# Attention followed by two dense layers: splits and value products put behind given instructions of their own engine

## The chip, the cores and the metric

One core of a Trainium2 chip. The kernel is one program; the metric is device time in microseconds, the median of several executions. The profile is one execution of its own, taken by the hardware profiler. Engines are named as in the profile: PE is TensorE (PEld its weight loads), DVE is VectorE, ACT is ScalarE, POOL is GpSimd, SP is SyncE, which here only issues transfers.

## The reference

Attention with a mask by hash bucket, and two dense blocks behind it:

```
q_bits = (q @ proj > 0); k_bits = (k @ proj > 0)          # 6 bits a row
mask   = bucket(q_bits) == bucket(k_bits)
scores = where(mask, q @ k.T / sqrt(64), -1e9)
attn   = softmax(scores); x = attn @ v                    # 2 batches, 8 heads, 768 rows, 64 wide
h  = x @ w_in;  g  = where(h > 0, h, exp(min(h, 0)) - 1);  x2 = g @ w_out     # 1536 x 512, inner 2048
h2 = x2 @ w_in2; g2 = s * relu(h2)**2 + b;                 out = g2 @ w_out2
```

## The kernel before

All large products keep the precision of 32 bits by splitting an operand into a high and a low 16-bit part and adding three products. The weights arrive as 64-bit numbers and are joined to 32-bit words on DVE (lines 213, 214, 216, one chunk is these three), then split (lines 205, 206, 221, 223).

The attention works in units. A unit is one head and 128 query rows: `u_s` makes its 128 x 768 scores on PE (line 384), `u_soft` takes their maximum on DVE (395, 396) and the exponential on ACT (397), `u_split` and `u_av` multiply by the values. There are 96 units; 16 of them are the first two chunks of rows, which `unit` orders so that units 0 to 3 are chunk 0 of heads 0 to 3, units 4 to 7 chunk 1 of the same heads, and units 8 to 15 the same for heads 4 to 7. For these 16, `u_split` transposes the exponentials on PE (line 406, six matmuls of 32-bit data), copies them out (line 409 on ACT), and `u_av` multiplies them with the raw 32-bit values (line 434). From unit 16 on the exponentials are split into two halves on ACT (416) and POOL (419), transposed by a DMA from SP (421), and multiplied with split values (440).

Heads come in four pairs. Before a pair's first unit its keys and queries are split by `p_split` (lines 280 or 282 the high part, 297 a copy, 285 the remainders), transposed by DMAs (303, 304, 312), hashed by `p_bits` (matmuls of line 340, comparison on DVE in line 343) and turned into buckets by `p_buck` (353, 357). `p_v` splits a pair's values for the units from 16 on (323 on ACT, 324 on DVE). Score tiles have one PSUM buffer in this stage, so a unit's scores wait for the maximum of the unit before.

What runs when is set in two steps. The tables at the head of the file (`SPLIT0`, `BITS0`, `PV0`, `LOADV`) say behind which unit a step is written by `attention`, and the order in which the program is written gives every instruction a priority. A scheduler then builds each engine's queue from the priorities and its own estimate of times. Each engine works its queue in order, so an instruction that waits holds up all behind it. `tc.issue_after(x)` adds one constraint: what is written inside it stands behind `x` in the queue of `x`'s engine.

Alongside, `w_stream` brings the first layer's weights; `moe1` (574, 582 to 597) starts on the first two chunks when both are normalised by `u_norm` and transposed (479). From then on matmuls of the first layer alternate with attention units, and after the attention only dense layers are left.

Of the kernel before, what the change touches and what calls it, by code (L numbers as in the profile page):

```python
# [19 lines left out]
EX = dict(p=1, ph=1, pt=1, raw=2)  # L20
NP = 3
LOAD = [(-1, -1), (0, 0)]
SPLIT0 = [(-4, -4), (-3, -3), (1, 1), (2, 3)]
ENG0 = ['dve', 'act', 'act', 'act']
MXP = 44
BITS0 = [-2, -1, 4, 6]
BUCK0 = [1, 0, 1, 1]
LOADV = [1, 2, 5, 6]
WN = 1
# [34 lines left out]
W_FROM = 3  # L64
HOLD = {(0, 2, "v"): 3, (0, 3, "v"): 4, (1, 0, "k"): 8, (1, 0, "q"): 9}
HOLD_E = []
LN2 = 0.6931471805599453


def model_kernel(tc, q, k, v, proj, w_in, w_out, w_in2, w_out2, s2, b2, sel, pop, eye, out):  # L70
    nc = tc.nc
# [23 lines left out]
    with ExitStack() as base:  # L95
# [194 lines left out]
        def p_split(b, hp, nm, eng):  # L290
            t = raws.pop((b, hp, nm)).rearrange("p h (c d) -> p h c d", d=D)
            s_ = ring.take("ph", [128, 2, C, 2, D], F16, "src")
            full = lambda z: z.rearrange("p h c t -> p (h c) t")
            if nm == "k":
                hi = s_[:, :, :, 0, :]
                scaled(eng, hi, t, SQ)
                side(b, hp).tensor_copy(out=s_[:, :, :, 1, :], in_=hi)
                l_ = ring.take("ph", [128, C, 2, D], F16, "srcl")
                for j in range(2):
                    rest(l_[:, :, j, :], t[:, j], SQ, hi[:, j])  # L300
                o1 = per.tile([128, 2, C, 128], F16, tag=f"k1{hp}", name=f"k1{hp}")
                o2 = per.tile([128, 2, C, 128], F16, tag=f"k2{hp}", name=f"k2{hp}")
                nc.sync.dma_start_transpose(out=full(o1), in_=s_.rearrange("p h c x d -> p (h c x d)"))
                nc.sync.dma_start_transpose(out=o2[:, 0], in_=l_.rearrange("p c x d -> p (c x d)"))
                k1[b, hp], k2[b, hp] = o1, o2
                return
            for j in range(2):
                hi, lo = s_[:, j, :, j, :], s_[:, j, :, 1 - j, :]
                scaled(eng, hi, t[:, j], -SQ)
                rest(lo, t[:, j], -SQ, hi)  # L310
            o1 = per.tile([128, 2, C, 128], F16, tag=f"q1{hp}", name=f"q1{hp}")
            nc.sync.dma_start_transpose(out=full(o1), in_=s_.rearrange("p h c x d -> p (h c x d)"))
            o2 = per.tile([128, 2, C, 128], F16, tag=f"q2{hp}", name=f"q2{hp}")
            for j in range(2):
                side(b, hp).tensor_copy(out=o2[D * j:D * j + D, j], in_=o1[D * j:D * j + D, j])
            q1[b, hp], q2[b, hp] = o1, o2

        def p_v(b, hp):
            t = raws[b, hp, "v"]
            vv = per.tile([128, 2, C, 2, D], F16, tag=f"vv{hp}", name=f"vv{hp}")  # L320
            hi, lo = vv[:, :, :, 0, :], vv[:, :, :, 1, :]
            t = t.rearrange("p h (c d) -> p h c d", d=D)
            nc.scalar.activation(out=hi, in_=t, func=ACTF.Copy, scale=SV)
            nc.vector.scalar_tensor_tensor(out=lo, in0=t, scalar=SV, in1=hi, op0=ALU.mult, op1=ALU.subtract)
            vHL[b, hp] = vv

# [51 lines left out]
        def u_s(u):  # L378
            b, c, h, hp, j = unit(u)
            p = ps_s[0].tile([128, S], F32, tag="s", name="s")  # L380
            for x, (w, m) in enumerate(((q1, k1), (q2, k2))):
                kf = m[b, hp][:, j].rearrange("p c t -> p (c t)")
                for a0, a1 in halves:
                    nc.tensor.matmul(p[:, a0:a1], w[b, hp][:, j, c, :], kf[:, a0:a1],  # L384
                                     start=(x == 0), stop=(x == 1))
            sps[u] = p

        def u_soft(u):
            b, c, h, hp, j = unit(u)
            gr, sl = group(u)  # L390
            if sl == 0:
                sums[gr] = sml.tile([128, H], F32, tag="sum", name="sum")
            f = ring.take("p", [128, S], F32, "p")
            mx = sml.tile([128, 1], F32, tag="mx", name="mx")
            nc.vector.tensor_scalar(f, sps.pop(u), CLAMP, None, op0=ALU.min, op1=ALU.min, accum_out=mx)  # L395
            (nc.gpsimd if U0 <= u < MXP else nc.vector).tensor_scalar(mx, mx, sm / (SQ * SQ), 10.0 * LN2, op0=ALU.mult, op1=ALU.add)  # L396
            nc.scalar.activation(out=f, in_=f, func=ACTF.Exp, scale=-sm / (SQ * SQ), bias=mx,  # L397
                                 accum_out=sums[gr][:, sl:sl + 1])
            pf[u] = f

        def u_split(u, eng):
            f = pf.pop(u)
            if u < FC * H:
                p = ps_p[0].tile([128, S], F32, tag="s", name="pT")
                for cc in range(C):
                    nc.tensor.transpose(p[:, 128 * cc:128 * cc + 128], f[:, 128 * cc:128 * cc + 128], ident)  # L406
                o = ring.take("pt", [128, S], F32, "pt")
                if eng == "act":
                    nc.scalar.activation(out=o, in_=p, func=ACTF.Copy)
# [14 lines left out]
        def u_av(u):  # L424
# [6 lines left out]
            if u < FC * H:  # L431
                vv = raws[b, hp, "v"].rearrange("p h (c d) -> p h c d", d=D)
                for cc in range(C):
                    nc.tensor.matmul(acc, o[:, 128 * cc:128 * cc + 128], vv[:, j, cc, :],  # L434
                                     start=(cc == 0), stop=(cc == C - 1))
                return
            vv = vHL[b, hp]
            for z, (x, y) in enumerate(((0, 0), (0, 1), (1, 0))):
# [587 lines left out]
```

## Time and profile before

| | |
|---|---|
| median of 3 runs | 711.56 us (709.78 to 711.82) |
| profiled execution, its own time | 714.04 us |
| its span in the trace | 711.8 us |
| PE busy | 659.6 us, 93% of the span |
| DVE busy | 520.5 us, 73% |
| ACT busy | 416.3 us, 58% |
| POOL busy | 266.1 us, 37% |

The shares are means over stages with different limits; the span is read stage by stage, in forty slices of 17.8 us and in windows. The granted clock is a share of TensorE's full 2.4 GHz, so 0.50 is its lower level of 1.2 GHz. "Idle before" in brackets names what ended an engine's wait.

### The profile page before, as it was taken

The numbers are of one execution on the slowest core, as the hardware profiler recorded it, in microseconds if no ns is written. First come the engines' busy times: TensorE is split into PE (matmuls) and PEld (weight loads), VectorE is DVE, ScalarE is ACT, GpSimd is POOL, SyncE is SP. The second block draws the span as 40 slices with busy tenths as digits, with TensorE's granted clock in tenths as the row PEclk, the third lists the DMA queues.
The fourth block names the chain that finished last, engine by engine and source line by source line (L and its number), as shares of the span: only waits on it lengthen the run. The fifth ranks groups of instructions, "written<-read, shape, count | busy, mean of one in ns | idle before, by whom it ended". The sixth has DMA issues, their size and how long they took to land.

```text
span 711.8 us, 15212 instructions
## 1 busy us (share of the span) xinstructions
PE 659.6 (93%) x6192; PEld 506.6 (71%) x6192; DVE 520.5 (73%) x893; ACT 416.3 (58%) x687; POOL 266.1 (37%) x211
## 2 busy tenths in 40 slices
PE   2598978879989999999999999999999999999998
PEld 0286857668767777888888988874444446888887
DVE  5779989998878568645644699339999626999730
ACT  2849768966778788656755333234545525555520
POOL 0136767776345469945855421311211200000000
PEclk9769999999999999999999999999999999999999
DMA  9965699999999669977668555014443000000100
GB/s 211 299 162 170 160 203 203 223 228 225 196 211 216 116 116 171 150 125 122 119 115 117 135 162 165 1 31 119 135 138 112 0 1 1 16 31 31 45 30 30
DMA packets 206805, 89.72 MB, mean 126 GB/s; under 512 B 171920, under 2 KB 203408, under 8 KB 206736
## 3 DMA queue, kind: packets, MB, share of 16 engines
q1 hardware_dynamic: 206144, 88.63, 57.4%
q8 instruction: 48, 0.79, 0.5%
q14 instruction: 21, 0.17, 0.1%
q10 hardware_dynamic: 592, 0.14, 0.1%
HBM read 43.13 MB, written 3.15 MB: 65 GB/s over the span
## 4 chain that ended last, share of the span: by engine, by line
PE 66%; DMA 10%; DVE 10%; ACT 7%; issue 5%; SPq 1%; POOL 1%; DVEq 0%; ACTq 0%; POOLq 0%
PE h L574 27%; PE y L818 15%; PE x2p L574 12%; DMA pt<-ph 6%; PE s L384 4%; PE xacc L440 3%; PE xacc L434 2%; DVE p L395 2%; ACT p L397 1%; PE pT L406 1%; ACT ph L416 1%; DMA q<-src 1%; DVE g L591 1%; DMA raw<-in_k 1%; ACT q L357 1%
## 5 line engine op out<-in xcount | busy, mean ns | idle before, releaser
L419 POOL TENSOR_TENSOR ph<-p,ph 128x768 f16<-128x768 f32 x80 | 134.6, 1686 | 79.2 <-ACT ph L416 44.3
L574 PE MATMUL h<-x,wih 128*128 128x256 f16 x768 | 131.3, 275 | 3.0 <-DVE g L591 1.5
L574 PE MATMUL h<-x,wi 128*128 128x512 f16 x576 | 124.5, 379 | 0.0
L395 DVE TENSOR_SCALAR_CACHE_REDUCE p<-s 128x768 f32<-128x768 f32 x96 | 91.0, 951 | 42.2 <-PE s L384 41.3
L397 ACT ACTIVATE p<-p,mx 128x768 f32<-128x768 f32 x96 | 89.2, 929 | 50.6 <-DVE mx L396 38.8
L818 PE MATMUL y<-wqh,a 128*128 128x256 f16 x672 | 110.3, 273 | 0.0
L818 PEld LDWEIGHTS <-a 128*128 128x128 f16 x1008 | 98.6, 98 | 11.7
L574 PE MATMUL h<-x,wil 128*128 128x256 f16 x384 | 105.4, 275 | 0.0
L574 PE MATMUL x2p<-gh,woh 128*128 128x256 f16 x384 | 104.1, 273 | 0.8 <-ACT gh L594 0.8
L574 PE MATMUL x2p<-gl,woh 128*128 128x256 f16 x384 | 104.5, 273 | 0.1
L574 PEld LDWEIGHTS <-wi 128*128 128x128 f16 x576 | 56.4, 98 | 67.7
L574 PE MATMUL x2p<-gh,wol 128*128 128x256 f16 x384 | 104.5, 273 | 0.0
L818 PE MATMUL y<-wql,a 128*128 128x256 f16 x336 | 91.1, 273 | 0.0
L384 PE MATMUL s<-k,q 128*128 128x512 f16 (+1 forms) x384 | 80.7, 335 | 8.0 <-DVE p L395 7.9
L574 PEld LDWEIGHTS <-wih 128*128 128x128 f16 x768 | 74.9, 99 | 15.2 <-issue 2.0
L574 PEld LDWEIGHTS <-woh 128*128 128x128 f16 x768 | 74.9, 98 | 11.6
L597 POOL TENSOR_TENSOR gl<-g,gh 128x512 f16<-128x512 f32 x48 | 59.0, 1229 | 61.0 <-ACT gh L594 60.7
L440 PE MATMUL xacc<-vv,pt 128*128 128x64 f16 x1440 | 57.6, 194 | 16.1 <-DMA pt<-ph 16.1
L416 ACT ACTIVATE ph<-p 128x768 f16<-128x768 f32 x80 | 66.7, 836 | 7.7 <-DMA pt<-ph 5.2
L440 PEld LDWEIGHTS <-pt 128*128 128x128 f16 x1440 | 53.5, 99 | 24.3 <-DMA pt<-ph 20.3
L610 DVE SCALAR_TENSOR_TENSOR g<-h,sbs,r 128x512 f32<-128x512 f32 x48 | 35.7, 745 | 23.6 <-ACT r L607 23.6
L384 PEld LDWEIGHTS <-q 128*128 128x128 f16 x384 | 34.5, 100 | 25.6 <-issue 10.8
(118 smaller groups left out, 1040.8 us busy)
## 6 DMA issues: line engine op xcount, KB each, us to landing
wraw<-in_moe_w_in SPq DMA_DIRECT2D x32, 512.0 KB, 3.9
wraw<-in_moe_w_out SPq DMA_DIRECT2D x32, 512.0 KB, 3.9
out<-y SPq DMA_DIRECT2D x10, 256.0 KB, 2.0
raw<-in_k SPq DMA_DIRECT2D x6, 384.0 KB, 4.8
raw<-in_q SPq DMA_DIRECT2D x6, 384.0 KB, 5.7
v<-in_v SPq DMA_DIRECT2D x4, 384.0 KB, 7.8
pt<-ph SPq DMA_TRANSPOSE x80, 4.1
x<-in_k SPq DMA_DIRECT2D x2, 384.0 KB, 5.0
```

What stands on the lines that cost most here:

```text
L357: nc.scalar.activation(out=o[r, j].rearrange("p c t -> p (c t)"), in_=p[r], func=ACTF.Relu, scale=sc, bias=pop_sb[r, x:x + 1])
L384: nc.tensor.matmul(p[:, a0:a1], w[b, hp][:, j, c, :], kf[:, a0:a1], start=(x == 0), stop=(x == 1))
L395: nc.vector.tensor_scalar(f, sps.pop(u), CLAMP, None, op0=ALU.min, op1=ALU.min, accum_out=mx)
L397: nc.scalar.activation(out=f, in_=f, func=ACTF.Exp, scale=-sm / (SQ * SQ), bias=mx, accum_out=sums[gr][:, sl:sl + 1])
L416: nc.scalar.activation(out=t[:, 0, :], in_=f, func=ACTF.Copy)
L419: nc.gpsimd.tensor_tensor(out=t[:, 1, :], in0=f, in1=t[:, 0, :], op=ALU.subtract)
L434: nc.tensor.matmul(acc, o[:, 128 * cc:128 * cc + 128], vv[:, j, cc, :], start=(cc == 0), stop=(cc == C - 1))
L440: nc.tensor.matmul(acc, o[:, C * x + cc, :], vv[:, j, cc, y, :], start=(z == 0 and cc == 0), stop=(z == 2 and cc == C - 1))
L574: nc.tensor.matmul(p, ws[a](kk), xs[b](kk), start=(kk == 0 and z == 0), stop=(kk == n_kk - 1 and z == 2))
L597: nc.gpsimd.tensor_tensor(out=gl, in0=t["g"], in1=gh, op=ALU.subtract)
L610: nc.vector.scalar_tensor_tensor(out=g, in0=p, scalar=sb["s"], in1=t["r"], op0=ALU.mult, op1=ALU.mult)
L818: nc.tensor.matmul(p, a[:, xa, kk, :], wq[y][:, WQ[n], kk, :], start=first and k == 0, stop=k == 3 * K2 - 1, skip_group_check=True)
```

## The change

The fourth pair's splits are written behind units 4 and 5 instead of 2 and 3, and its bits one unit later. Five constraints are added: its key split stands behind the exponential of unit 1, the first half of its query split behind that of unit 2; the value splits of the first two pairs behind the exponentials of units 4 and 5; the value product of unit 0 behind the transposes of unit 2, and that of unit 1 behind the scores of unit 4. To be named in a constraint, exponentials, scores and transposes are kept in `pins`.

```diff
-SPLIT0 = [(-4, -4), (-3, -3), (1, 1), (2, 3)]
+SPLIT0 = [(-4, -4), (-3, -3), (1, 1), (4, 5)]
...
-BITS0 = [-2, -1, 4, 6]
+BITS0 = [-2, -1, 4, 7]
...
+HOLD_V = {0: 4, 1: 5}
+HOLD_A = {0: ("pT", 2), 1: ("s", 4)}
+HOLD_S = {(0, 3, "k"): 1, (0, 3, "q"): 2}
...
+            u_ = HOLD_S.get((b, hp, nm))
+            held = tc.issue_after(pins["exp", u_]) if u_ is not None else nullcontext()
             if nm == "k":
                 hi = s_[:, :, :, 0, :]
-                scaled(eng, hi, t, SQ)
+                with held:
+                    scaled(eng, hi, t, SQ)
...
             for j in range(2):
                 hi, lo = s_[:, j, :, j, :], s_[:, j, :, 1 - j, :]
-                scaled(eng, hi, t[:, j], -SQ)
+                with held if j == 0 else nullcontext():
+                    scaled(eng, hi, t[:, j], -SQ)
...
-            nc.scalar.activation(out=hi, in_=t, func=ACTF.Copy, scale=SV)
+            with tc.issue_after(pins["exp", HOLD_V[hp]]) if b == 0 and hp in HOLD_V else nullcontext():
+                nc.scalar.activation(out=hi, in_=t, func=ACTF.Copy, scale=SV)
...
                 for cc in range(C):
-                    nc.tensor.matmul(acc, o[:, 128 * cc:128 * cc + 128], vv[:, j, cc, :],
-                                     start=(cc == 0), stop=(cc == C - 1))
+                    with tc.issue_after(pins[HOLD_A[u]]) if u in HOLD_A and not cc else nullcontext():
+                        nc.tensor.matmul(acc, o[:, 128 * cc:128 * cc + 128], vv[:, j, cc, :],
+                                         start=(cc == 0), stop=(cc == C - 1))
```

The scheduler carries the change into all queues. Three places follow; names carry the program's buffer numbers, and the change's line numbers are 3 to 9 higher than those of the kernel before.

ACT, from the second pair's buckets on, before. `p` are exponentials (291 and 334 are units 0 and 1, 395 unit 2), `raw_296` and `raw_298` the fourth pair's keys and queries, `vv0` to `vv3` the value splits of the four pairs, `pt` the copied transposes:

```order
L357 ACTIVATE q21_199<-pone_267,pop_sb_112 64x768 x2
L280 ACTIVATE src_402<-raw_296 128x12x64
L397 ACTIVATE p_291,sum_290<-p_291,mx_292 128x768
L280 ACTIVATE src_451<-raw_298 128x6x64 x2
L323 ACTIVATE vv0_850<-v0_339 128x12x64
L323 ACTIVATE vv1_879<-v0_400 128x12x64
L397 ACTIVATE p_334,sum_290<-p_334,mx_335 128x768
L206 ACTIVATE wih_154<-wa_283 128x512
L409 ACTIVATE pt_317<-pT_310 128x768
L409 ACTIVATE pt_378<-pT_371 128x768
```

And with the change (395, 436 and 475 are units 2, 3 and 4):

```order
L365 ACTIVATE q21_199<-pone_267,pop_sb_112 64x768 x2
L405 ACTIVATE p_291,sum_290<-p_291,mx_292 128x768
L405 ACTIVATE p_334,sum_290<-p_334,mx_335 128x768
L209 ACTIVATE wih_154<-wa_283 128x512
L283 ACTIVATE src_572<-raw_298 128x6x64
L417 ACTIVATE pt_317<-pT_310 128x768
L405 ACTIVATE p_395,sum_290<-p_395,mx_396 128x768
L417 ACTIVATE pt_378<-pT_371 128x768
L283 ACTIVATE src_572<-raw_298 128x6x64
L417 ACTIVATE pt_419<-pT_412 128x768
L209 ACTIVATE wih_154<-wa_302 128x512
L405 ACTIVATE p_436,sum_290<-p_436,mx_437 128x768
```

The fourth pair's key split (`raw_296`) and the first two value splits have gone from among the first exponentials; units 0 and 1 now follow each other, and one half of the query split stands ahead of unit 2. The key split comes again after unit 4 and the first pair's value split (`vv0`), seven rows below this piece's last.

PE from the first transpose to the third pair's bit products, weight loads left out, before. `pT` are the transposes, `s` the scores (four matmuls a unit, of which one stands here), `xacc` the value products, six a unit:

```order
L406 MATMUL pT_310<-ident_109,p_291 128x128 x6
L406 MATMUL pT_371<-ident_109,p_334 128x128 x6
L384 MATMUL s_431<-k11_188,q11_197 128x512
...
L434 MATMUL xacc_543<-v0_339,pt_317 128x64 x6
L434 MATMUL xacc_543<-v0_339,pt_378 128x64 x6
L406 MATMUL pT_422<-ident_109,p_395 128x128 x6
L384 MATMUL s_480<-k10_168,q10_177 128x512
...
L434 MATMUL xacc_543<-v0_400,pt_429 128x64 x6
L406 MATMUL pT_471<-ident_109,p_446 128x128 x6
```

And with the change:

```order
L414 MATMUL pT_310<-ident_109,p_291 128x128 x6
L414 MATMUL pT_371<-ident_109,p_334 128x128 x6
L392 MATMUL s_421<-k11_188,q11_197 128x512
...
L414 MATMUL pT_412<-ident_109,p_395 128x128 x6
L443 MATMUL xacc_533<-v0_339,pt_317 128x64 x6
L392 MATMUL s_460<-k10_168,q10_177 128x512
...
L443 MATMUL xacc_533<-v0_339,pt_378 128x64 x6
L443 MATMUL xacc_533<-v0_400,pt_419 128x64 x6
L414 MATMUL pT_451<-ident_109,p_436 128x128 x6
```

The first value product stands behind the third transpose, the second behind the fifth scores (`s_460`). In both, the third pair's bit products come next.

SP at the transposes of the first x block, second half (`x0` from `xh_1029`), before:

```order
L421 DMA_TRANSPOSE pt_967<-ph_964 128x12x128
L421 DMA_TRANSPOSE pt_994<-ph_991 128x12x128
L175 DMA wraw_1178<-in_moe_w_out 128x4x256
L479 DMA_TRANSPOSE x0_113<-xh_1029 128x4x128 x2
L421 DMA_TRANSPOSE pt_1015<-ph_1012 128x12x128
L421 DMA_TRANSPOSE pt_1092<-ph_1089 128x12x128
L421 DMA_TRANSPOSE pt_1140<-ph_1137 128x12x128
```

And with the change:

```order
L429 DMA_TRANSPOSE pt_967<-ph_964 128x12x128
L429 DMA_TRANSPOSE pt_994<-ph_991 128x12x128
L488 DMA_TRANSPOSE x0_113<-xh_1029 128x4x128
L429 DMA_TRANSPOSE pt_1015<-ph_1012 128x12x128
L488 DMA_TRANSPOSE x0_113<-xh_1029 128x4x128
L178 DMA wraw_1281<-in_moe_w_out 128x4x256
```

One transpose of exponentials (`pt_1015`) has moved between the two that x needs, and a weight load has moved ahead.

## Rows read from the trace of the kernel before

**Rows 1.** The page's forty slices of 17.8 us: busy tenths, and granted clock.
```profile
PE   2598978879989999999999999999999999999998
...
DVE  5779989998878568645644699339999626999730
...
PEclk9769999999999999999999999999999999999999
```

**Rows 2.** Windows: us, then each engine's busy time, granted clock, DMA share, GB/s.
```profile
20.00:30.00 10.00, 4.39 (x19) 1.35 (x16) 7.90 (x17) 7.26 (x12) 1.49 (x1) 0.75 1.15 326
30.00:40.00 10.00, 8.33 (x37) 7.26 (x38) 9.69 (x20) 6.08 (x11) 2.82 (x2) 0.50 1.15 216
40.00:50.00 10.00, 10.00 (x60) 7.53 (x60) 5.06 (x10) 4.82 (x8) 2.65 (x2) 0.56 0.68 206
50.00:60.00 10.00, 7.97 (x74) 5.82 (x72) 9.95 (x20) 9.36 (x14) 6.24 (x4) 1.00 0.35 100
...
90.00:100.00 10.00, 6.71 (x54) 4.70 (x54) 9.57 (x18) 6.96 (x13) 7.76 (x9) 0.83 0.82 181
```

**Rows 3.** Order of time, ACT: start, duration, line, operation, idle before.
```profile
28.07 0.83 ACT L280 ACTIVATE src<-raw 128x768 f16<-128x768 f32 x1
28.80 0.92 ACT L397 ACTIVATE p<-p,mx 128x768 f32<-128x768 f32 x1
...
29.72 0.92 ACT L280 ACTIVATE src<-raw 128x384 f16<-128x384 f32 x2
...
32.01 0.92 ACT L397 ACTIVATE p<-p,mx 128x768 f32<-128x768 f32 x1
...
33.45 0.79 ACT L409 ACTIVATE pt<-pT 128x768 f32<-128x768 f32 x1
...
35.70 0.94 ACT L397 ACTIVATE p<-p,mx 128x768 f32<-128x768 f32 x1 [0.23 <-DVE mx L396]
```

**Rows 4.** Order of time, PE, from the first transpose to the bits.
```profile
29.87 1.54 PE L406 MATMUL pT<-ident,p 128*128 128x128 f32 x6 [1.71 <-ACT p L397]
33.08 1.54 PE L406 MATMUL pT<-ident,p 128*128 128x128 f32 x6 [1.67 <-ACT p L397]
...
40.70 1.49 PE L406 MATMUL pT<-ident,p 128*128 128x128 f32 x6
41.98 1.49 PE L384 MATMUL s<-k,q 128*128 128x512 f16 x4
...
47.13 0.61 PE L340 MATMUL pbit<-k,pjkhl 128*32 128x512 f16 x2
```

**Rows 5.** Groups by line on DVE, 0 to 165 us: busy, mean ns, idle before.
```profile
L213 DVE TENSOR_SCALAR wx<-wraw 128x512 int32<-128x512 int32 x29 | 20.0, 690 | 0.3
...
L591 DVE SCALAR_TENSOR_TENSOR g<-h,e 128x512 f32<-128x512 f32 x8 | 5.4, 681 | 2.1 <-ACT e L584 2.1
...
L285 DVE SCALAR_TENSOR_TENSOR srcl<-raw,src 128x384 f16<-128x384 f32 x8 | 4.1, 549 | 0.0
...
L315 DVE COPY q<-q 64x768 f16<-64x768 f16 x8 | 3.6, 444 | 3.6 <-DMA q<-src 3.5
...
L297 DVE COPY src<-src 128x768 f16<-128x768 f16 x4 | 1.4, 360 | 1.7 <-ACT src L280 1.7
```

**Rows 6.** Windows of one microsecond at the clock's fall and return.
```profile
25.00:26.00 1.00, 0.06 (x1) 0.00 (x0) 1.00 (x4) 0.99 (x2) 0.00 (x0) 0.50 1.07 372
...
48.00:49.00 1.00, 1.00 (x16) 0.42 (x8) 0.00 (x0) 0.79 (x2) 0.59 (x1) 0.55 0.73 193
```

**Rows 7.** Order of time, SP: two transposes of exponentials in its queue.
```profile
92.20 4.46 SPq L421 DMA_TRANSPOSE pt<-ph  x2
```

**Rows 8.** Waits of PE, 100 to 290 us: total, times, longest.
```profile
PE xacc L440 <- DMA pt<-ph: 14.0, 13, 2.4
...
PE h L574 <- DMA x<-xh: 1.5, 1, 1.5
```

**Rows 9.** Key tiles, up to 70 us: the transposes' time to landing.
```profile
DMA to landing us min/median/max: 3.2/4.5/9.4
```

More of the change, by code (lines that the diff above doesn't have):

```diff
@@ L383, in u_s @@
                 for a0, a1 in halves:
-                    nc.tensor.matmul(p[:, a0:a1], w[b, hp][:, j, c, :], kf[:, a0:a1],
-                                     start=(x == 0), stop=(x == 1))
+                    pins["s", u] = nc.tensor.matmul(p[:, a0:a1], w[b, hp][:, j, c, :], kf[:, a0:a1],
+                                                    start=(x == 0), stop=(x == 1)).ins
             sps[u] = p
@@ L396, in u_soft @@
             (nc.gpsimd if U0 <= u < MXP else nc.vector).tensor_scalar(mx, mx, sm / (SQ * SQ), 10.0 * LN2, op0=ALU.mult, op1=ALU.add)
-            nc.scalar.activation(out=f, in_=f, func=ACTF.Exp, scale=-sm / (SQ * SQ), bias=mx,
-                                 accum_out=sums[gr][:, sl:sl + 1])
+            pins["exp", u] = nc.scalar.activation(out=f, in_=f, func=ACTF.Exp, scale=-sm / (SQ * SQ), bias=mx,
+                                                  accum_out=sums[gr][:, sl:sl + 1]).ins
             pf[u] = f
@@ L405, in u_split @@
                 for cc in range(C):
-                    nc.tensor.transpose(p[:, 128 * cc:128 * cc + 128], f[:, 128 * cc:128 * cc + 128], ident)
+                    pins["pT", u] = nc.tensor.transpose(p[:, 128 * cc:128 * cc + 128], f[:, 128 * cc:128 * cc + 128], ident).ins
                 o = ring.take("pt", [128, S], F32, "pt")
```

## Prediction

> **What bounds the kernel now.** I read the page's forty slices first, then windows of ten microseconds, then the order of time on single engines.
>
> The slices [rows 1] split the run in two. From the thirteenth slice on (213 us) TensorE (PE) is at 9 in every slice, and the nearly 500 us that are left are mostly matmuls that this change does not touch. Before that PE has holes, and VectorE (DVE) stands at 9 in five of the six slices from 53 to 160 us. So the first stage is a DVE stage, with one exception at its start, and the windows [rows 2] show it: from 20 to 50 us DVE is busy 7.90, 9.69 and 5.06 of each 10 us, so it stands for 2.10 + 0.31 + 4.94 = 7.35 us; from 50 us on it has next to no gap. In the same stretch the granted TensorE clock is 0.75, 0.50 and 0.56. From 40 to 50 us PE is busy all the time at half clock and DVE waits for it: there the first attention units bound the kernel through PE, and the change is made just there.
>
> What holds PE up is ScalarE (ACT). The first exponential starts at 28.80, behind the fourth pair's key split of 28.07; the second only at 32.01, behind that pair's query split and two value splits [rows 3]. So PE begins the first transpose at 29.87, waits 1.67 us for the second (33.08), and from there runs without a gap to the third pair's bit products at 47.13 [rows 4].
>
> **The change, part by part.** No arithmetic is added or removed: the same instructions stand in another order, and the constraints are between instructions of one engine. The sum is made against the profiled execution, 714.04 us; the median of the runs is 711.56, and I carry the difference over to it.
>
> *Splits behind exponentials (ACT).* The key split leaves the place before the first exponential, which then starts at 28.07 instead of 28.80: 0.73 us. The second follows at 28.07 + 0.92 = 28.99 instead of 32.01. The third stands behind one weight copy, half a query split (0.46) and one copy of a transposed tile (0.79): it starts at about 31.8 instead of 35.70. Only the first half of the fourth pair's query split is held behind the third exponential; the other half goes ahead of it, which costs those 0.46 us and is in this figure.
>
> *PE up to the third pair's bits.* From the first transpose to the bit products PE now takes 47.13 - 29.87 = 17.26 us. The work is one transpose, 41.98 - 40.70 = 1.28, and the gapless 47.13 - 33.08 = 14.05, so 15.33 us at half clock; the changed order holds the same work in that stretch. Starting 0.73 us earlier, at 29.14, and without gaps it reaches the bits at 44.47: **2.66 us earlier**. The gaps stay away only if each transpose finds its exponential: the second is wanted at 30.4 and its exponential ends at 29.9; the third at 33.0, its exponential ends at 32.7. It is tight, not late.
>
> *The held value products.* The first goes behind the third transpose, the second behind the fifth scores. On PE this is neutral (same work before the bits), but the fifth scores now run after one value product instead of two, so DVE gets them earlier and can fill the hole of 40 to 50 us. I give this nothing of its own: it is how DVE can follow the 2.66.
>
> *DVE at the third pair's bits.* By that instruction the changed order has done one weight chunk more (three instructions of about 0.69, 2.07) and not yet the fourth pair's copy (0.36), two key remainders (1.10), key copy (0.36, taken as the other) and two query copies (0.89), together 2.71 [rows 5]. So DVE arrives 2.66 earlier but owes 0.64: its lead is **2.0 us**. From there to 160 us it is the engine with hardly a gap, so the lead lasts.
>
> *The stall before the first gate product.* At 108 us DVE stands 2.1 us for the first layer's exponential, with the first g in its queue [rows 5]. In the changed order that g stands behind one more weight subtraction and the unit's score maximum, so other work covers part of it; against that, the second half of the first x block waits on SyncE behind one more transpose (4.46 for two, 2.2 us each) [rows 7], and PE already waits 1.5 us for x [rows 8]. Bounds: 0 and 2.1; no row is nearer to one end, and I take half, **1.0 us**.
>
> *Value splits of pairs 1 and 2 behind the fifth and sixth exponential; everything after 115 us.* The value remainders are wanted only from the seventeenth unit, after 90 us, so their delay is covered. Later rows of all queues are shuffled by one or two places; I count zero, with the cover that DVE, then PE, is busy; without it each such wait is worth up to 2.4 us, the longest of the waits for transposed exponentials [rows 8].
>
> Sum: 2.0 + 1.0 = 3.0 us, 711.0 for the profiled execution and **708.6 us** for the median.
>
> **The rivals.**
>
> *The clock comes back earlier.* The granted clock fell to 0.50 at 25 us, in a stretch in which PE was busy 4.39 of 10 us [rows 2], and was back between 48 and 49 us, after the unbroken work from 33.08 and just after the bits began [rows 4, 6]. In the changed order PE works unbroken from 29.14. If that brings the clock back before the bits, PE needs up to half of 14 us less, and DVE's 7.35 us of gaps bound the gain: 2.66 of them are in my sum, 4.7 are left. Time: 708.6 - 4.7 = 703.9. Against it: in the kernel before, 13 us of unbroken work stayed at half, and the work ahead of the bits is the same. The Trainium skill (TensorE: Matmul & The Clock Gate, Part 1: The HAM clock gate) says that the throttled state is the default and activity releases it; by that the clock would return in the middle of the transposes and value products, and the run would take this rival's time; this trace does not agree, since it held 0.50 through them. Chance 0.12.
>
> *The lead is swallowed later.* Between 100 and 290 us PE stands 14.0 us in 13 waits for transposed exponentials [rows 8]. They end with ACT, GpSimd and the transfers, not with DVE; if these, in their shuffled order, take as long to come, an earlier DVE only waits. One or two longer waits of 1 to 2.4 us eat the 3.0. Time about 711, anything from 709.5 to 712.5. For it: every queue is shuffled from here on; against it: what feeds those chains is the scores' maximum on DVE, which comes earlier. Chance 0.25.
>
> *The fourth pair comes late (slower).* Its key split leaves 28.07 for a place behind the fifth exponential, about 45 us. On DVE the third pair's bits begin at 46.5; the copy and the key remainders end some 6.2 us on, and about 6.6 us of other work lies between them and the copy of the fourth pair's second key tile, which stands ahead of the ninth unit's scores. In these 6.6 us there must be one weight word (0.7), one load's issue (about 0.5) and the transpose to landing: 4.5 in the median [rows 9], so 5.7, and 0.9 us are to spare. At the longest landing, 9.4, DVE stands 4.0 us, PE behind it; a PE gap of that kind brought 3.4 us of half clock between 90 and 100 us (0.83 of ten) [rows 2], 1.7 us of work lost. Together 5.7 - 3.0 = 2.7 slower: 714.3. It decides from a landing of 5.4 us, and turns the sign from 8.4 or, with the clock, 6.7. Against it: most key transposes of the kernel landed sooner. Chance 0.15.
>
> *The constraints do nothing.* In the built order all of them hold except half a query split, as said above; that is in the sum.
>
> **How the numbers follow.** Forecast 0.48, clock 0.12, swallowed 0.25, fourth pair 0.15. A measurement of this kernel can tell about 0.3%, 2.1 us. Faster by more: 0.44 of the forecast and the clock's 0.12, 0.56. Within: 0.04 of the forecast, 0.22 of the swallowed, 0.03 of the fourth pair, 0.29. Slower: 0.03 + 0.12 = 0.15. Range: from a little under the clock's bound, 703.0, up to 713.3, which leaves out the worst of the fourth pair's cases.
>
> **What would show it.** In the changed profile: first exponential at about 28.1 and the next right behind; PE without a gap from 29 us; the third pair's bits on PE near 44.5 and on DVE near 46.5; granted clock 0.50 until then; DVE's standing time from 20 to 50 us cut from 7.35 to about 5; the first x product near 97 to 98 us as before or up to 1 us earlier, but the end of the first stage, where PE's slices turn to 9, about 3 us earlier. Wrong would be: half clock ended long before the bits (clock), a DVE wait before the fourth pair's key copy at 57 to 60 us (fourth pair), or the bits early while PE's waits for transposed exponentials add up to well over 14 us (swallowed).

## The result, and the profile after

The changed kernel takes **722.65 us** (median of 4 runs, 720.09 to 723.81) beside 711.69 us of the kernel before on the same chip (4 runs, 709.78 to 713.87): ratio **1.0148**, 95% interval 1.0105 to 1.0191, some 11 us slower, where 3 us faster was forecast. The profiled execution has a span of 719.4 us against 711.8. Line numbers of the changed kernel are 3 to 9 higher (its L405 is L397 before, L414 is L406, L283 is L280), those of the crossed kernels further down one more. One execution of the control below took 2070.90 us and one of the kernel before beside it 1748.09 us; both are left out, and the control was profiled a second time.

The page's slices, as in [rows 1]:

```profile
PE   2598969879887999999999999999999999999998
...
DVE  5879799878869567845644599529999726999730
...
PEclk9767989999999999999999999999999999999999
```

PE is at 9 throughout from the fourteenth slice on, as before from the thirteenth. The windows that answer to [rows 2] (us, busy time of PE, PEld, DVE, ACT, POOL, granted clock, DMA share, GB/s):

```profile
30.00:40.00 10.00, 8.01 (x41) 6.87 (x39) 8.15 (x19) 5.50 (x11) 5.46 (x4) 0.67 1.13 302
40.00:50.00 10.00, 10.00 (x68) 7.83 (x68) 6.69 (x10) 6.62 (x10) 4.65 (x3) 0.63 0.67 104
50.00:60.00 10.00, 8.24 (x62) 6.03 (x60) 8.99 (x21) 9.21 (x14) 4.42 (x3) 0.83 0.62 127
60.00:70.00 10.00, 8.33 (x60) 6.56 (x59) 9.66 (x21) 7.12 (x10) 6.43 (x6) 0.89 0.69 222
70.00:80.00 10.00, 9.59 (x63) 8.41 (x64) 7.10 (x16) 6.90 (x13) 5.66 (x6) 0.77 0.52 133
```

In this execution the half clock is not one stretch that ends before 50 us, as in [rows 2], but several, up to 75 us. ACT in order of time, for [rows 3]:

```profile
27.20 0.92 ACT L405 ACTIVATE p<-p,mx 128x768 f32<-128x768 f32 x1
...
28.12 0.92 ACT L405 ACTIVATE p<-p,mx 128x768 f32<-128x768 f32 x1
...
31.28 0.52 ACT L283 ACTIVATE src<-raw 128x384 f16<-128x384 f32 x1 [1.27 <-DMA k<-src]
31.71 0.79 ACT L417 ACTIVATE pt<-pT 128x768 f32<-128x768 f32 x1
32.40 0.92 ACT L405 ACTIVATE p<-p,mx 128x768 f32<-128x768 f32 x1
```

PE in order of time, for [rows 4], and DVE at the two pairs' places:

```profile
28.45 2.38 PE L414 MATMUL pT<-ident,p 128*128 128x128 f32 x12
30.67 0.81 PE L392 MATMUL s<-k,q 128*128 128x512 f16 x4
33.47 1.35 PE L414 MATMUL pT<-ident,p 128*128 128x128 f32 x6 [1.99 <-ACT p L405]
...
44.78 0.61 PE L348 MATMUL pbit<-k,pjkhl 128*32 128x512 f16 x2
...
54.18 1.44 PE L392 MATMUL s<-k,q 128*128 128x512 f16 x4 [1.76 <-DVE p L403]
...
67.66 1.40 PE L414 MATMUL pT<-ident,p 128*128 128x128 f32 x6 [1.25 <-ACT k L365]
```
```profile
46.93 0.96 DVE L351 TENSOR_SCALAR bits<-pbit 128x768 f16<-128x768 f32 x1 [2.20 <-PE pbit L348]
...
58.84 0.58 DVE L354 COPY k<-k 64x768 f16<-64x768 f16 x1 [0.69 <-DMA k<-srcl]
```

The first two exponentials are close together, the bits leave PE at 44.78 instead of 47.13, and DVE reaches them at 46.93, 2.3 us earlier than before (49.18). But PE stands 1.99 us for the third exponential at 31.5 to 33.5, and the windows of one microsecond (for [rows 6]) show the clock on either side of that hole:

```profile
30.00:31.00 1.00, 1.00 (x9) 0.86 (x8) 1.00 (x5) 0.01 (x1) 0.91 (x1) 0.85 1.24 313
...
32.00:33.00 1.00, 0.00 (x0) 0.00 (x0) 1.00 (x2) 1.00 (x2) 0.83 (x1) 1.00 1.24 291
...
34.00:35.00 1.00, 1.00 (x7) 1.00 (x5) 0.80 (x3) 0.67 (x3) 0.00 (x0) 0.50 1.28 289
```

It had come back to full before 31 us, while PE worked from 27.2 on; after the hole it is at 0.50 again, and stays there until 47 us. The Trainium skill (TensorE: Matmul & The Clock Gate, Part 1: The HAM clock gate) says that activity releases the throttled state; here the trace agrees, where in the prediction the profile of before did not. A second profile of the changed kernel, in the third group of experiments, meets the same hole without the fall.

SyncE, for [rows 7], and PE's waits from 100 to 290 us, for [rows 8]:

```profile
101.64 1.52 SPq L488 DMA_TRANSPOSE x<-xh  x1
103.66 1.69 SPq L429 DMA_TRANSPOSE pt<-ph  x1
105.41 1.32 SPq L488 DMA_TRANSPOSE x<-xh  x1
```
```profile
PE xacc L449 <- DMA pt<-ph: 15.5, 16, 3.0
PE pbit L348 <- DMA q<-src: 1.2, 1, 1.2
PE pone L361 <- DVE bits L351: 1.2, 2, 0.9
PE pbit L348 <- DMA k<-src: 1.2, 1, 1.2
PE h L583 <- DVE g L600: 1.1, 1, 1.1
PE s L392 <- ACT k L365: 1.1, 2, 0.7
PE pone L361 <- DVE p L403: 0.9, 1, 0.9
```

**Where the time went.** I summed PE's busy time times granted clock, in windows of 2 us, to the work that it had done by a point in time. What is missing of elapsed time is idle time, or time lost to the half clock.

| work done by | 50 us | 80 | 160 | 320 | idle by 320 | lost to the clock by 320 |
|---|---|---|---|---|---|---|
| before | 19.3 | 46.0 | 110.7 | 259.4 | 48.0 | 12.6 |
| before, profiled again | 19.0 | 44.8 | 110.7 | 257.9 | 46.3 | 15.8 |
| changed | 20.1 | 41.6 | 103.9 | 251.1 | 51.9 | 17.0 |
| changed, profiled again | 21.2 | 41.7 | 104.5 | 247.3 | 57.3 | 15.3 |

A lead at 50 us is there in both, but it is no larger than what one order differs by from execution to execution: in two more profiles with the early queues of the kernel before, those of the control and of a crossed kernel below, 22.8 and 24.7 us are done by then. By 60 us the lead is gone, and it has turned into some 3 to 4 us less work by 80 us (those two have 46.8 and 46.9 there, and a crossed kernel with the changed early queues has 45.2); the rest, some 4 us in the first profile, more in the second, is lost between 80 and 310 us. From there on both kernels run alike, the changed one 7.6 us later in the first profiles. So two questions: what takes the early part, and what the later one.

### The profile page after: what moved, and what is told of

Its sections match the earlier page's. It is cut to its first block, busy times and chain, and to the rows that moved or that the text cites. A ratio compares the mean times of both kernels' runs of the same rounds, so it can differ in the third digit from the quotient of the medians.

```text
span 719.4 us, 15214 instructions
## 1 busy us (share of the span) xinstructions
PE 663.3 (92%) x6192; PEld 510.2 (71%) x6192; DVE 523.6 (73%) x893; ACT 416.1 (58%) x687; POOL 263.9 (37%) x211
## 4 chain that ended last, share of the span: by engine, by line
PE 56%; ACT 3%; DVE 3%; DMA 1%; issue 1%; POOL 0%; DVEq 0%; ACTq 0%; POOLq 0%
PE h L583 25%; PE y L827 15%; PE x2p L583 11%; PE s L392 3%; PE xacc L449 3%; DMA pt<-ph 1%; DVE e L598 1%; ACT p L405 1%; ACT gh L603 1%; DVE p L403 1%; DVE g L600 1%; ACT ph L424 1%; ACT e L591 0%; ACT k L365 0%; POOL ph L427 0%
## 5 line engine op out<-in xcount | busy, mean ns | idle before, releaser
L427 POOL TENSOR_TENSOR ph<-p,ph 128x768 f16<-128x768 f32 x80 | 132.7, 1662 | 84.2 <-ACT ph L424 56.6
L405 ACT ACTIVATE p<-p,mx 128x768 f32<-128x768 f32 x96 | 89.2, 929 | 54.3 <-DVE mx L404 46.2
L449 PE MATMUL xacc<-vv,pt 128*128 128x64 f16 x1440 | 57.8, 195 | 15.6 <-DMA pt<-ph 15.5
L449 PEld LDWEIGHTS <-pt 128*128 128x128 f16 x1440 | 53.4, 99 | 25.7 <-DMA pt<-ph 21.4
```

Source lines behind the costliest of these rows:

```text
L405: pins["exp", u] = nc.scalar.activation(out=f, in_=f, func=ACTF.Exp, scale=-sm / (SQ * SQ), bias=mx, accum_out=sums[gr][:, sl:sl + 1]).ins
L427: nc.gpsimd.tensor_tensor(out=t[:, 1, :], in0=f, in1=t[:, 0, :], op=ALU.subtract)
L449: nc.tensor.matmul(acc, o[:, C * x + cc, :], vv[:, j, cc, y, :], start=(z == 0 and cc == 0), stop=(z == 2 and cc == C - 1))
```

## The experiments

Theory F put the early loss, and the late one with it, on the fourth pair's lateness; P on the held value products; V on the held value splits; S on the order of the later queues, which the program's scheduler works out anew for every kernel, so that any change moves hundreds of instructions after 100 us. Medians are set against the kernel before on the same chip (710.23 to 711.90 us in the five groups of runs).

**1. The holds one by one.** The changed kernel with one part taken back; the first two edits are

```diff
 e1: the fourth pair as before, the other holds kept
-SPLIT0 = [(-4, -4), (-3, -3), (1, 1), (4, 5)]
+SPLIT0 = [(-4, -4), (-3, -3), (1, 1), (2, 3)]
-BITS0 = [-2, -1, 4, 7]
+BITS0 = [-2, -1, 4, 6]
-HOLD_S = {(0, 3, "k"): 1, (0, 3, "q"): 2}
+HOLD_S = {}
 e2: the fourth pair alone
-HOLD_V = {0: 4, 1: 5}
-HOLD_A = {0: ("pT", 2), 1: ("s", 4)}
+HOLD_V = {}
+HOLD_A = {}
```

and the third and fourth empty `HOLD_A` alone, and `HOLD_V` alone.

> The changed kernel with the fourth pair's splits and bits back where they stood before; the held value splits and the held value products stay. Theory F (the late fourth pair makes PE's gaps and with them the half clock of 50 to 80 us, and the late first x block): no half clock between 50 and 80 us, the pair's bits on PE near 55 us, the time 709 to 714 us, so 8 to 13 us under the changed kernel's 722.65. Theory P (the held value products cost): half clock between 50 and 80 us as in the changed kernel, 719 to 724. Theory S (any new order of the later queues costs some microseconds, between 100 and 310 us): the half clock is gone, but PE's idle time by 320 us is still 2 to 4 us over that of the kernel before (48.0), 714 to 718.

> Only the fourth pair's splits are held and its bits come one step later; value splits and value products as in the kernel before. Theory F: half clock between 50 and 80 us costs 3 to 5 us as in the changed kernel, 718 to 724 us. Theory P: near the kernel before or ahead of it, 708 to 713. Theory S: between, 713 to 719, with idle time after 100 us that is not that of the changed kernel.

> The changed kernel without the holds on the first two value products. Theory P: back to 709 to 713 us, without half clock between 50 and 80 us. Theory F: 718 to 724, half clock between 50 and 80 us as in the changed kernel. Theory S: anything from 712 to 722.

> The changed kernel without the holds on the value splits of the first two pairs, so that they stand again before the second exponentials' successors on ACT. Theory V (the held value splits crowd ACT between 45 and 60 us and delay the relus of the fourth pair): 710 to 714 us. Theory F: 718 to 724, since the fourth pair is as late. Theory S: 712 to 722.

Measured: the fourth pair back 715.53 us (ratio 1.0071, 1.0042 to 1.0100); fourth pair alone 717.22 (1.0108, 1.0059 to 1.0158); no held products 720.68 (1.0143, 1.0098 to 1.0188); no held value splits 726.19 (1.0225, 1.0180 to 1.0270). V falls: without its hold the kernel is slower still, and slower than any theory said. With the fourth pair back 7.1 us return, where F said 8 to 13, and a half-clock stretch (53.7 to 57.1 us) is still there; the time is in S's range, though PE's idle time by 320 us, 53.7, is above the 50 to 52 that S implied. The fourth pair alone is in S's range and just below F's. The third run does not fit P by its time, while the work of its early part does: PE had 47.7 us done at 80 us, against 41.6 in the changed kernel, and stood idle for 5.5 us between 120 and 130 us instead. None of the four comes near the kernel before.

**2. One hold at a time, one place, and a control.** The kernel before with `HOLD_V` alone, with `HOLD_A` alone, with `HOLD_S = {(0, 3, "k"): 0, (0, 3, "q"): 1}` alone, and as a control with none of them but

```diff
-SC0 = 1.2
+SC0 = 1.15
```

> The kernel before with only the value splits of the first two pairs held behind the fifth and sixth exponential. Theory H (each hold has a price of its own): the two holds left in the first experiment (715.53 us, 4.6 over the kernel before) share it out, so that this one or the next carries the 4 to 5 us and the other stands within 1.5 us of the kernel before. Theory S (every new order of the later queues costs, whatever made it): this one and the next both 713 to 717 us, with PE's idle time by 320 us at 51 to 54 us against 48.0 before.

> The kernel before with only the first two value products held, behind the third transpose and the fifth scores. Theory H: this one or the one before carries the 4 to 5 us, the other is within 1.5 us of the kernel before. Theory S: 713 to 717 us, PE's idle time by 320 us at 51 to 54 us.

> The kernel before with the fourth pair's splits moved by one place only: the key split behind the first exponential, the query split behind the second; the places of its bits and buckets in the program's order stay, and value splits and products are not held. The first exponential comes 0.7 us earlier. Theory F (the price is the fourth pair's lateness): its copy, remainders and bits are where they stood, so none of the 6 us of the second experiment, 708 to 712 us. Theory S: 713 to 717 us, as every new order.

> A control: the kernel before with one constant of the interleave of the first layer and attention 4% lower (1.15 for 1.2). All queues are as before until 119 us; behind that hundreds of instructions stand at other places, as in every kernel of this study. Theory S: 712 to 716 us, PE's idle time by 320 us 2 to 4 us over that of the kernel before. Theories F and H: 709 to 712.5 us, since nothing near the fourth pair, the value splits or the first products is touched.

Measured: value splits alone 719.95 us (1.0105, 1.0067 to 1.0142); products alone 718.45 (1.0086, 1.0058 to 1.0114); one place 716.74 (1.0073, 1.0047 to 1.0100); the control 714.68 (1.0030, 1.0007 to 1.0052). H's numbers fail, since the two holds cost about 8 and 6.5 us alone and 4.6 together; F's fail too, since the one-place move costs 5 us although nothing of the pair is late. Every order so far is slower than that of before, and in the control some 2 us (0.5 to 3.7 by its interval) come without any edit ahead of 119 us. S has the one-place move and the control within its ranges, but not the two holds alone: both take longer than its 713 to 717, and with less idle time by 320 us (50.5 and 49.3) than its 51 to 54.

**3. Second profiles, and half the lateness.** The kernel before, the changed kernel and the control once more, and the changed kernel with `SPLIT0` and `BITS0` of before but all holds kept.

> The kernel before, profiled a second time: its first profile had a mean granted clock of 0.978 and 714.0 us, while its runs beside the experiments have 0.985 in the mean and 711.5 us. Theory D (the ends of the half-clock stretches differ from one execution of the same order to the next): the stretch that began at 25 us ends elsewhere than at 49, between 33 and 47, and PE's idle time by 320 us grows by part of what the clock loses less. If the stretches belong to the order: the same three stretches, 25 to 49, 96 to 100 and 161 to 165 us.

> The changed kernel, profiled a second time. Theory F: the gaps of PE at 52 to 54 and 66 to 70 us and half-clock stretches within 2 us behind each stand there again, whatever the stretch before 50 us does; idle by 320 us 51 to 54 us. Theory D alone: the gaps stay but the half clock behind them comes and goes.

> The control, profiled again because its first profile was of a disturbed execution. Theory S: until 119 us the places of PE's gaps are those of the kernel before, and idle time between 120 and 320 us is 2 to 4 us over that of the kernel before in its second profile; clock losses as there. Otherwise its 2 us come from the clock.

> The changed kernel with the fourth pair's step numbers (splits 2 and 3, bits 6) as before, but all holds kept: its splits stand between the third and the fourth exponential instead of between the third and the sixth, and its relus again behind the ninth and tenth exponential. Theory F: half the lateness, so the clock's loss is 11 to 14 us instead of 17.8, and the time 715 to 719 us. Theory S: 714 to 724 us, without a relation to the fourth pair's place.

Measured: 715.57, 725.55 and 714.61 us in one run each, and 718.14 us (1.0111, 1.0061 to 1.0160). In the changed kernel PE's holes at 52 to 54 and 67 to 71 us stand again (at 53.5 and at 67.5 and 70.0) with half clock at the first and behind the last; so does the hole at 31.5. Its idle time by 320 us is 57.3, over F's 51 to 54. In the control, 120 to 320 us holds 18.8 us of idle time against 16.6 and 16.3 in the two profiles of before, 2 us more, as S said. The fourth kernel's time lies in F's range and in S's; its clock loss by 320 us, 15.3, is over F's 11 to 14. The kernel before has its three stretches of half clock again (25.7 to 49.6, 97 to 104 and 162 to 166 us) and a fourth at 56 to 60, against what D said of this profile.

One thing in the changed kernel's second profile matters for what follows. PE stands 1.67 us for the third exponential, up to 33.15, and the clock does not fall behind that hole: it is full until 44.4 us and falls at the end of a later wait of PE, 3.53 us for a copied transpose.

```profile
30.00:40.00 10.00, 8.33 (x78) 6.95 (x78) 7.79 (x18) 5.38 (x10) 5.11 (x4) 0.96 1.13 309
40.00:50.00 10.00, 6.47 (x37) 5.13 (x31) 8.91 (x13) 7.22 (x11) 4.72 (x3) 0.72 0.60 88
```

The work done by 80 us is the same as in the first profile, and the execution was the slower of the two (725.55 us against 721.52). So the half clock of 33 to 47 us in the first profile is no necessary part of what the change costs.

The window of 40 to 50 us, in the kernel before, the same again, and the control, whose queues are the same until 119 us:

```profile
40.00:50.00 10.00, 10.00 (x58) 7.55 (x58) 4.92 (x11) 4.81 (x8) 2.68 (x3) 0.52 0.69 201
```
```profile
40.00:50.00 10.00, 8.99 (x83) 6.97 (x82) 9.45 (x16) 9.04 (x14) 4.52 (x4) 1.00 0.66 202
```

The first row is the second profile of the kernel before (0.52, as in [rows 2]); in the control the clock is at full. So one order of the queues meets either clock there, and a single profile can't settle the early part. Times and repeated profiles have to.

**4. Crossing early and late.** To separate the two parts, these kernels take each engine's built order of one kernel up to the thirteenth unit's score maximum (about 75 us), and from there, instruction by instruction, the built order of another:

```python
held = set(order)                  # the other kernel's instructions from the cut on
for k, i in ins.items():
    if k not in held: after(ins[late[k[0]][0]], i)
for ks in late.values():           # one list for each engine
    for a, b in zip(ks, ks[1:]): after(ins[b], ins[a])
```

`ins` are the program's instructions, `late` the other kernel's from the cut on, by engine. `after(i, j)` queues i behind j on their engine, with no wait for its end. In the traces the queues follow the one kernel's order up to the cut and the other's behind it.

> Every engine's queue is that of the changed kernel up to the thirteenth unit's score maximum (about 75 us) and from there, instruction for instruction, that of the kernel before. Theory F (the price is in the early part, PE's gaps and half clock between 50 and 80 us): 719 to 724 us. Theory S (the price is in the later queues' order): 709 to 713 us. Both, about half each, as the work done by 80 us in the changed kernel's two profiles (4.2 and 4.4 us less than before) tells: 714 to 718 us.

> The other way round: the kernel before up to the thirteenth unit's score maximum, the changed kernel's queues from there. Theory F: 710 to 713 us. Theory S: 718 to 723 us. Both: 714 to 719 us, and this run's excess over the kernel before and that of the run before add up to about the 11 us of the whole change.

> The early queues of the experiment in which the fourth pair's splits move by one place only (PE had 3.2 us more work done at 80 us than in the kernel before), with the kernel before's queues from the thirteenth unit's score maximum on. Theory S: a lead is worth something only when the later queues stay: 708 to 711 us, ahead of the kernel before by 1 to 3. Theory F: 711 to 713, as the kernel before; if a lead is always lost: 711 to 714.

> The early queues of the changed kernel without the held value products (1.7 us more work done at 80 us than before, though the fourth pair is as late), with the kernel before's queues from the thirteenth unit's score maximum on. Theory S: 709 to 712 us instead of that experiment's 720.7. Theory F: 717 to 721, as that experiment.

Measured: early part changed, later part as before, 717.89 us (1.0091, 1.0062 to 1.0119); the reverse 719.38 (1.0123, 1.0089 to 1.0157); the one-place move with the later part of before 714.30 (1.0031, 1.0006 to 1.0056); no held products with the later part of before 713.70 (1.0034, 1.0013 to 1.0055). So both parts carry price: the early one 6.8 us, the later one 722.65 - 717.89 = 4.8 behind the changed early part and 8.3 behind that of before; they don't simply add up, as the second expectation had it. The last two runs miss as well: 714.30 us is over all three ranges, and 713.70 lies between S's and F's. And the later order that the scheduler made for an edited early part had the longer median wherever I compared them: 2.4 us for the one-place move, where the intervals overlap, and 7.0 us without the products.

Part of what the later order costs can be read off PE's waits from 75 to 320 us. In the kernel that is as before up to 75 us and has the changed kernel's later queues:

```profile
PE pbit L349 <- DMA q<-src: 1.6, 1, 1.6
PE pone L362 <- DVE bits L352: 1.4, 2, 1.1
...
PE s L393 <- ACT k L366: 1.2, 2, 0.9
...
PE pone L362 <- DVE p L404: 0.9, 1, 0.9
PE pbit L349 <- DMA k<-src: 0.9, 1, 0.9
```

These are the second batch's bits and buckets, between 185 and 244 us. They add up to 6.0 us here, and to 5.6 us in the changed kernel, which has the same five rows (above), as has its second profile. In the kernel before only the waits for `q<-src` and for the bits are there, 0.6 us each, and in the kernel of 711.30 us below, which has its later queues, 0.6 and 0.9. Which move in the queues brings them was not tried, and no run shows that the time follows these waits alone.

**5. The early price.** The kernel without held products and with the later queues of before (713.70 us) holds the fourth pair's splits just as the crossed one of 717.89 us does, and costs 4.2 us less; in the program they differ in the held value products. In both, ACT stands 1.6 to 1.7 us before half of the query split, ahead of the third exponential, for the half's buffer (31.28 in the rows of ACT above, 31.15 and 31.10 here; for the last the profile names no releaser). Without the hold PE does the first value product meanwhile; with it, it has nothing. Theory G says that this is the early price. One edit takes this wait away:

```diff
             for j in range(2):
                 hi, lo = s_[:, j, :, j, :], s_[:, j, :, 1 - j, :]
-                with held if j == 0 else nullcontext():
+                with tc.issue_after(pins["exp", u_]) if u_ is not None else nullcontext():
                     scaled(eng, hi, t[:, j], -SQ)
```

and another run leaves the fourth pair as before and keeps the held products, both with the later queues of before.

> The crossed kernel of 717.89 us (early queues of the changed kernel, later queues of the kernel before) with both halves of the fourth pair's query split held behind the third exponential, not only the first. Theory G (the early price is made at 31 to 33 us: the unheld half waits 1.3 to 1.4 us on ACT for a buffer ahead of the third exponential, the first value product is held behind the third transpose, so PE has nothing else, stands 2 us, and the clock that had just come back falls for up to 14 us): PE's gap at 31.5 to 33.5 and the half clock of 33 to 47 us are gone, 713 to 715 us. Otherwise (the lateness of the pair's bits between 55 and 70 us makes it): 716.5 to 719 us.

> The early queues of the first experiment (the fourth pair as before, value splits and products held), the later queues of the kernel before. Theory G: the fourth pair's query split stands whole ahead of the second exponential, there is no stall of 2 us with the clock just back, 712 to 714.5 us. If the held products cost by themselves: 716 to 719 us.

Measured: **711.30 us (0.9994, 0.9976 to 1.0013)** with both halves held, 6.6 us under the kernel that it was made of; 713.64 (1.0039, 1.0020 to 1.0057) with the fourth pair back. ACT, PE and two windows of the first:

```profile
30.76 0.94 ACT L406 ACTIVATE p<-p,mx 128x768 f32<-128x768 f32 x1
...
32.38 0.92 ACT L284 ACTIVATE src<-raw 128x384 f16<-128x384 f32 x2
```
```profile
31.84 0.88 PE L415 MATMUL pT<-ident,p 128*128 128x128 f32 x6 [0.24 <-ACT p L406]
32.55 1.45 PE L444 MATMUL xacc<-v,pt 128*128 128x64 f32 x12
```
```profile
30.00:40.00 10.00, 8.78 (x82) 7.32 (x81) 7.43 (x17) 6.12 (x11) 5.31 (x4) 0.97 1.14 310
40.00:50.00 10.00, 6.73 (x29) 5.04 (x29) 9.96 (x18) 7.37 (x12) 4.45 (x3) 0.71 0.43 96
```

and the same places in the kernel with one half held (717.89 us):

```profile
31.15 0.52 ACT L284 ACTIVATE src<-raw 128x384 f16<-128x384 f32 x1 [1.72 <-DMA k<-src]
```
```profile
33.34 0.88 PE L415 MATMUL pT<-ident,p 128*128 128x128 f32 x6 [1.65 <-ACT p L406]
```

With both halves held the third exponential starts at 30.76 instead of 32.27 and the transpose waits 0.24 us instead of 1.65. The clock is at 0.97 in the window of 30 to 40 us, where it was 0.67, but the half clock is not gone: it stands at 44.2 to 51.1 us, behind holes of 1.90 and 2.35 us. The time fell below G's range, and the later queues are the same in both kernels, so the early price hangs on where that one half stands in the program.

That the wait at 31 to 33 us is the price is not shown by it. The scheduler built the early queues anew for this edit, and other places moved with it. On DVE the sixth unit's score maximum and the fourth pair's key copy, with one half held:

```profile
48.30 0.94 DVE L404 TENSOR_SCALAR_CACHE_REDUCE p<-s 128x768 f32<-128x768 f32 x1
...
57.78 0.46 DVE L355 COPY k<-k 64x768 f16<-64x768 f16 x1 [0.81 <-DMA k<-srcl]
```

and with both:

```profile
45.70 0.94 DVE L404 TENSOR_SCALAR_CACHE_REDUCE p<-s 128x768 f32<-128x768 f32 x1
...
54.48 0.36 DVE L355 COPY k<-k 64x768 f16<-64x768 f16 x1 [0.41 <-DMA k<-srcl]
```

With both held, the sixth maximum stands ahead of a value remainder and a query copy that came before it, and the key copy ahead of another value remainder. So the fourth pair is no longer late: its bits reach DVE at 58.08 us instead of 60.82 (59.31 in the kernel before). And the wait that Theory F named, PE behind the pair's relus on ACT, is there with one half held and not with both:

```profile
66.48 0.88 PE L415 MATMUL pT<-ident,p 128*128 128x128 f32 x6 [1.25 <-ACT k L366]
```

In time, the kernel with one half held is not behind after its hole: it starts the fifth maximum at 37.63 us, the other at 39.91. It falls behind by 2.6 us at the sixth, and by 5.0 us at the thirteenth (75.54 against 70.53). So the loss of these two profiles is made between 38 and 75 us, where the lateness of the fourth pair and the new queue places act as well. To tell them apart, the early queues of the one kernel would have to be kept, instruction for instruction, with that half alone moved; no run does it. A single profile is weak evidence besides: in four profiles with the early queues of the kernel before the thirteenth maximum starts between 71.50 and 76.34.

In the run with the fourth pair back, the held products and value splits together cost 2.4 us (1.4 to 4.1 by the interval). No kernel of this study is measurably faster than the kernel before.

## Why the prediction was wrong

- **The early exponentials** came out as said: the first 1.6 us earlier (0.73 forecast; ACT's relus ahead of it also ended earlier in this execution), the second right behind.
- **The third exponential** is the first row that came out otherwise. The prediction put half a query split (0.46) ahead of it, start 31.8, and said of the transposes: "It is tight, not late." That half also had to wait 1.27 us for a buffer, which a row of time on ACT alone could not show since the split stood elsewhere before; the exponential started at 32.40. And PE wanted it earlier than at half clock, because the clock was back by 31 us. So PE stood 1.99 us. With the other half held too the early price of 6.8 us is gone but for 0.1; by what path, through this wait or through the queue places that moved with it, stays open.
- **PE at the bits** (44.47 forecast, 44.78 measured) and **DVE at the bits** (46.5, 46.93) are right by number and partly by luck: the stall of 2 us and faster transposes between 30 and 33 us cancel out. In the second profile, with the stall and at full clock, the bits leave PE at 39.18 and DVE takes them at 44.31; with both halves held it is 37.87 and 44.23.
- **"so the lead lasts"** is the step of the sum that failed: DVE came to the bits 2.25 us earlier (2.66 forecast), and nothing of that was left at the ninth unit. Its score maximum starts at 60.18, before at 60.17; the eleventh at 69.73, before at 67.04. The prediction drew the lead from DVE's busy share, as if DVE alone set the pace from 50 us on. In between PE waits for maxima (1.76 at 54.18) and for exponentials behind the fourth pair's relus on ACT (1.25 at 67.66), and in the first profile each hole is followed by half clock.
- **The stall before the first gate product**, counted as 1.0 us of gain: the wait itself went as forecast, from 2.1 us to nothing (the row below, for [rows 5]). But the transposes of the second half of the first x block start at 101.64 and 105.41 instead of 97.33 and 99.02, with another transpose between, the first x product at 102.20 instead of 98.05, and the first g at 113.78 instead of 108.14. The prediction named those transposes, and yet gave the term no bound below 0.

```profile
L600 DVE SCALAR_TENSOR_TENSOR g<-h,e 128x512 f32<-128x512 f32 x8 | 5.5, 685 | 0.0
```

- **"Later rows of all queues are shuffled by one or two places; I count zero"** is the other step that failed, a term put at nothing. The later order alone is worth 4.8 to 8.3 us, and that of the control, which changes nothing before 119 us, some 2. The price of a new order should have stood in the sum, with a sign: of the changed orders none was faster. The cover that was given, "that DVE, then PE, is busy", did not hold in the second batch, where PE waits for bits and buckets.
- **The rivals.** The fourth pair's lateness was priced by a DVE wait of up to 4.0 us at its key copy; that wait is 0.69 us (58.84). The pair's lateness may still act through the relus on ACT, which the rival did not name; the runs don't separate it, as said above. Its time came closest, and was still 8 us short. "Swallowed later" had the place right (100 to 290 us) and the releaser half wrong: the waits for transposed exponentials grew from 14.0 to 15.5 us only, those for the bits and buckets of the second batch from 1.2 to 5.6. "The clock comes back earlier" did happen, at 30.3 us, until the next hole; in the second profile it stayed until 44.4 us, and that execution took 725.55 us, so the gain of this rival did not follow either.

## What to carry to other kernels

When an instruction is moved behind another, look at every piece that is not moved with it: here half of a split stayed ahead and waited for a buffer, and a second constraint had taken away the work that covered such waits. Where a scheduler builds the queues, an early edit also buys a new later order, so cross the early queues of one kernel with the later ones of the other before blaming either, and put a price on the new order in the forecast. An experiment that edits the program there gets new queues too, so compare the queues before calling it one edit. A gain that depends on one profile's half clock is to be checked against a second profile.

## What the runs showed that I had not expected

The same queues met a different clock from one execution to the next. In two profiles of the kernel before, the half clock that begins at 25 us lasted until 49 and 50 us; in the control and in the crossed kernel with the same early queues it ended at 37.2 and 37.1 us (0.64 and 0.65 in the window of 30 to 40 us, 1.00 in the next). The kernel before has a mean granted clock between 0.973 and 0.998 in its runs, and times from 706.90 to 716.24 us. The time follows the clock less than I thought: two runs at 0.993 took 715.41 and 715.04 us, one at 0.995 took 709.83. That fits the windows of 40 to 50 us above, where VectorE is busy 4.92 us at half clock and 9.45 at full: behind them PE waits 2.61 us for a maximum in the control (51.84), 1.42 us in the kernel before (55.84 and 56.37). The Trainium skill (TensorE: Matmul & The Clock Gate, Part 1: The HAM clock gate) says that the number of matmuls at the low clock differs between runs of one kernel; these profiles agree, and show it in the middle of the first stage, not at its start alone.
